# Query weights split over two DMA queues, keys and queries of two tiles up front, and x tile 2 loaded behind the weights

## Chip, cores, metric

One core of a Trainium2 chip runs the whole program. The metric is the device time of one execution in microseconds (us); a lower one is better. A profile is one execution; its times count from the start of the span. Most runs of one kernel agree within 0.3%, so a few tenths of a microsecond mean something only as a median over several runs.

The five engines here are TensorE (PE, matmuls; PEld is its weight load), VectorE (DVE), ScalarE (ACT), GpSimd (POOL) and SyncE (SP). Two of them issue DMA transfers (copies between memories, done by 16 DMA engines) in this kernel: SyncE, whose transfers the profile lists as queue q1, and ScalarE, queue q10.

## The reference

```python
# x: (1, 2048, 640) bf16, 32 heads of 20
g = sigmoid((x * gate_w).sum(-1))
q, k, v = split(x @ wqkv)                    # wqkv: (640, 1920)
phi = lambda t: where(t > 0, t + 1, exp(t)) + 1e-6
kv  = einsum(phi(k), v);  z = phi(k).sum over tokens
a   = (phi(q) @ kv) / (phi(q) . z + 1e-6) @ wo
b   = (gelu(x @ w_gate) * (x @ w_up)) @ w_down     # 1728 wide
out = g * a + (1 - g) * b
```

Only the first stage matters here: keys and queries of the 16 token tiles (128 tokens each), that is, x times wk and x times wq. Both weights are cut into five chunks of 128 rows (`k` = 0 to 4), 160 KB each. TensorE needs x transposed; tile 0 is transposed by TensorE, all the others by DMA on their way in.

## The kernel before

The start of the load program. Each operation is put on the queue of its engine in this order; waits are derived from what is read and written.

```python
NQ = 4        # tiles whose keys and queries are computed apart
...
load_x(0)                 # SyncE: x tile 0, plain
load_wk(0)                # SyncE
load_xT(1)                # SyncE: x tile 1, transposed by DMA
load_wk(3); load_wk(4)    # SyncE
load_wk(1, "act"); load_wk(2, "act")     # ScalarE
...
for i in range(2, NQ):    # SyncE: x tiles 2 and 3, transposed
    load_xT(i)
for k in range(KC):       # SyncE: wq, five chunks
    load_wq(k)
for i in range(NQ, NT):   # SyncE: x tiles 4 to 15, transposed
    load_xT(i)
# ... then plain x, gate and up weights, wv, wo
```

TensorE's program in the first stage: `KM(n, ks)` accumulates keys, `QM(n, ks)` queries, over the chunks `ks`, each chunk as two matmuls (512 and 128 or 129 columns). `seq` lists the keys of the NQ tiles, then their queries. After that `KQ(i)` does keys and queries of one tile together, three matmuls per chunk (512, 512, 257 columns). I call `KM`/`QM` the split form and `KQ` the fused form.

```python
warm(5, 512); warm(1, 128)               # matmuls on constants
T(0, [0], 7); T(0, [1, 2, 3, 4], 6)      # transpose x tile 0
warm(2, 128)
for k in range(3): KM(0, [k])
for k in range(3): KM(1, [k])
KM(0, [3]); KM(1, [3]); gate_col(); KM(0, [4]); KM(1, [4])
for n in range(2 * NQ):
    if n in (2, 3):
        KM(n, ALLK)                      # keys of tiles 2, 3
    if n == NQ:
        for k in ALLK:                   # queries of two tiles, chunk by chunk
            QM(NQ, [k]); QM(NQ + 1, [k])
    if n > NQ + 1:
        QM(n, ALLK)
    phi1(n); phi2(n)                     # ScalarE and VectorE
for i in range(NQ, NT):
    KQ(i)
    ...
```

## Time and profile before

| | before |
|---|---|
| time, median of 6 runs beside the change | 273.90 us (273.52 to 274.20) |
| span of the profiled run | 272.6 us |
| TensorE busy | 267.6 us (98%) |
| keys of tiles 0 and 1: first matmul / last ends | 4.45 / 7.7 us |
| key matmuls of tile 2 start | 8.12 us |
| first fused tile (tile 4) starts | 16.3 us |
| stage after the fused tiles starts | 48.80 us |

The page of the kernel before, its head, TensorE's line, and the chain of work that ended last:

```profile
span 272.6 us, 3416 instructions
...
PE 267.6 (98%) x1341; PEld 127.9 (47%) x1367; DVE 140.8 (52%) x247; ACT 75.9 (28%) x132; POOL 30.0 (11%) x28
...
PE 96%; DMA 1%; SPq 1%; issue 1%; DVE 0%
```

TensorE bounds the kernel. Its waits, from the list of who waited for whom (total us, times, longest us):

```profile
PE ps L419 <- PEq L914: 0.8, 1, 0.8
PE ps L453 <- DMA pool<-in_A_wqkv_dram: 0.5, 1, 0.5
PE ps L453 <- DMA pool<-in_A_x_dram: 0.4, 1, 0.4
```

That is all: the start, the first key weights, and a transposed tile of x. The timeline of TensorE around the last (start, duration, engine, line, operation; in brackets the idle time before it and what ended it):

```profile
7.27 0.38 PE L453 MATMUL ps<-pool 128*128 128x512 bf16 x1
7.49 0.22 PE L454 MATMUL ps<-pool 128*128 128x128 bf16 x1
8.12 0.39 PE L453 MATMUL ps<-pool 128*128 128x512 bf16 x1 [0.42 <-DMA pool<-in_A_x_dram]
```

The next key matmul would have started at about 7.55 us, one step of 0.06 after 7.49; it started 0.57 us later. This is what the change can win.

SyncE's queue in the same run (start and total duration of issue, merged):

```profile
3.06 1.04 SPq L341 DMA_DIRECT2D pool<-in_A_wqkv_dram  x2
4.14 2.53 SPq L353 DMA_TRANSPOSE pool<-in_A_x_dram  x2
6.72 2.48 SPq L341 DMA_DIRECT2D pool<-in_A_wqkv_dram  x5
9.24 16.34 SPq L353 DMA_TRANSPOSE pool<-in_A_x_dram  x12
```

The two transposes stand between wk's last chunks and wq. A semaphore event is the signal that a part of a load has landed, and each load here has 16. When a load landed is read from the last of them in the trace: wk's last chunk at 6.83 us, x tile 2 at 8.07, tile 3 at 8.77, wq at 9.40, 10.13, 10.55, 11.54, 12.05.

### The profile page before, as it was taken

The page shows a single profiled execution, that of the slowest core. Times are in us where ns is not written, and L with a number is a line of the kernel's source. Part 1 is how long each engine was busy: PE and PEld are TensorE (multiplying, and loading weights), DVE is VectorE, ACT ScalarE, POOL GpSimd, SP SyncE. Part 2 cuts the span into 40 slices and gives each one's busy share as a digit, 9 for nine tenths or more (in the row PEclk, how much of TensorE's full clock was granted, in tenths as well). Part 3 has the DMA queues.
Part 4 walks back from the last instruction along what each step waited for, and adds up shares of the span by engine and source line. Part 5 has one row for each costly group of instructions (what it writes and reads, how often), then busy time and mean ns, then how long its engine had stood idle before and what let it go on. Part 6 is the DMA issues. An engine that isn't in the chain of part 4 may idle for free.

```text
span 272.6 us, 3416 instructions
## 1 busy us (share of the span) xinstructions
PE 267.6 (98%) x1341; PEld 127.9 (47%) x1367; DVE 140.8 (52%) x247; ACT 75.9 (28%) x132; POOL 30.0 (11%) x28
## 2 busy tenths in 40 slices
PE   8999999999999999999999999999999999999997
PEld 3555555544445454444444444444444444444444
DVE  1678989997233335999999999634210000000200
ACT  2455555210422453232222233224011122121021
POOL 5000000003240002242332422000000000000000
DMA  7976999600200011514121221273031110110211
GB/s 192 202 115 127 346 399 388 140 2 19 58 19 2 23 50 51 192 34 49 26 48 25 49 48 27 60 219 105 5 77 38 41 38 19 38 41 19 58 58 41
DMA packets 42864, 23.78 MB, mean 87 GB/s; under 512 B 32223, under 2 KB 41439, under 8 KB 42719
## 3 DMA queue, kind: packets, MB, share of 16 engines
q1 hardware_dynamic: 42517, 23.22, 31.9%
q10 hardware_dynamic: 330, 0.33, 0.3%
q8 instruction: 11, 0.18, 0.3%
q14 instruction: 6, 0.05, 0.1%
HBM read 13.83 MB, written 2.63 MB: 60 GB/s over the span
## 4 chain that ended last, share of the span: by engine, by line
PE 96%; DMA 1%; SPq 1%; issue 1%; DVE 0%
PE ps L700 41%; PE ps L864 23%; PE ps L539 12%; PE ps L596 6%; PE ps L843 4%; PE ps L468 2%; PE ps L811 2%; PE ps L678 2%; PE ps L599 1%; DMA pool<-in_A_x_dram 1%; PE ps L453 1%; PE ps L824 1%; SPq L341 1%; PE ps L721 1%; SPq L353 0%
## 5 line engine op out<-in xcount | busy, mean ns | idle before, releaser
L700 PE MATMUL ps<-pool 128*128 128x512 bf16 x510 | 113.0, 379 | 0.5
L700 PEld LDWEIGHTS ps<-pool 128*128 128x128 bf16 x520 | 50.5, 98 | 60.0
L864 PE MATMUL ps<-pool 128*128 128x512 bf16 (+2 forms) x300 | 62.4, 366 | 0.3
L706 ACT ACTIVATE pool<-ps 128x512 f32<-128x512 f32 x52 | 31.0, 597 | 73.1 <-PE ps L700 73.1
L708 DVE TENSOR_TENSOR pool<-ps,pool 128x512 bf16<-128x512 f32 x52 | 34.7, 689 | 31.7 <-PE ps L700 30.4
L864 PEld LDWEIGHTS ps<-pool 128*128 128x128 bf16 x306 | 29.2, 98 | 33.4 <-issue 0.4
L847 DVE TENSOR_TENSOR pool<-ps,pool 128x512 bf16<-128x512 f32 x4 | 2.8, 690 | 61.5 <-PE ps L843 61.5
L539 PE MATMUL ps<-pool 128*128 128x512 bf16 (+1 forms) x176 | 32.5, 343 | 0.2
L754 POOL TENSOR_TENSOR pool<-pool 128x640 f32<-128x640 bf16 x16 | 22.4, 1404 | 73.0 <-DVE pool L756 65.6
L871 ACT ACTIVATE pool<-ps,pool 128x512 bf16<-128x512 f32 (+1 forms) x16 | 10.9, 680 | 68.6 <-PE ps L864 68.6
L539 PEld LDWEIGHTS ps<-pool 128*128 128x128 bf16 x180 | 17.6, 98 | 15.0
L558 DVE SCALAR_TENSOR_TENSOR pool<-ps,pool 128x128 bf16<-128x128 f32 (+2 forms) x36 | 21.7, 602 | 2.1
L549 ACT ACTIVATE pool<-ps 128x640 bf16<-128x640 f32 x24 | 16.9, 703 | 15.8 <-DVE pool L558 9.3
L596 PE MATMUL ps<-pool 128*128 128x512 bf16 x76 | 19.2, 379 | 0.1
L764 DVE TENSOR_TENSOR pool<-pool 128x640 bf16<-128x640 bf16 x16 | 13.2, 826 | 0.6
L762 DVE TENSOR_SCALAR pool<-pool 128x32 f32<-128x32 f32 x16 | 12.8, 802 | 0.6
L756 DVE TENSOR_REDUCE pool<-pool 128x32 f32<-128x640 f32 x16 | 12.9, 808 | 0.0
L644 DVE TENSOR_TENSOR pool<-pool 128x640 f32<-128x640 f32 x14 | 11.6, 826 | 0.5
L843 PE MATMUL ps<-pool 128*128 128x512 bf16 x51 | 11.5, 379 | 0.1
L646 POOL PARTITION_ALL_REDUCE pool<-pool x1 | 4.0, 3971 | 61.0 <-DVE pool L644 61.0
L596 PEld LDWEIGHTS ps<-pool 128*128 128x128 bf16 x78 | 7.0, 98 | 7.3
L555 DVE TENSOR_SCALAR pool<-pool 128x640 bf16<-128x640 bf16 x24 | 7.9, 327 | 1.7 <-ACT pool L549 0.4
(70 smaller groups left out, 124.1 us busy)
## 6 DMA issues: line engine op xcount, KB each, us to landing
out_dram<-pool SPq DMA_DIRECT2D x19, 128.0 KB, 1.7
pool<-in_B_w_gate_dram SPq DMA_DIRECT2D x1, 2080.0 KB, 14.8
pool<-in_B_w_up_dram SPq DMA_DIRECT2D x1, 2080.0 KB, 18.0
pool<-in_A_wqkv_dram SPq DMA_DIRECT2D x8, 160.0 KB, 3.1
pool<-in_A_x_dram SPq DMA_DIRECT2D x1, 1280.0 KB, 9.2
pool<-in_A_x_dram SPq DMA_DIRECT2D x1, 1120.0 KB, 6.3
pool<-in_B_w_down_dram SPq DMA_DIRECT2D x1, 1120.0 KB, 6.4
pool<-omg_row SPq DMA_DIRECT2D x1, 1024.0 KB, 4.8
```

Of the source, the lines that this page charges most:

```text
L539: last = e.matmul(ps[:, b + p, 0:c1 - c0], xT[:, k, i * 128:(i + 1) * 128], wkq[:, k, c0:c1], start=(k == 0), stop=(k == KC - 1))
L549: P.op("act", lambda e: e.activation(e_buf[m], ps_flat[:, o:o + 640], ACT.Exp), reads=banks, writes=[r_e[m]])
L558: P.op("dve", lambda e, c0=c0, c1=c1: e.scalar_tensor_tensor(dst[:, c0:c1], ps_flat[:, o + c0:o + c1], 1.0 + EPS, e_buf[m][:, c0:c1], ALU. ...
L596: last = e.matmul(ps[:, b, :], pk[i][:, c * 128:(c + 1) * 128], x_aug[:, i, 0:512], start=(i == 0), stop=(i == NT - 1))
L700: last = e.matmul(ps[:, b, :], w[:, k, fc * 128:(fc + 1) * 128], xT[:, k, j * 512:(j + 1) * 512], start=(k == 0), stop=(k == KC - 1))
L706: P.op("act", lambda e: e.activation(ge[n], ps[:, gb, :], ACT.Gelu_apprx_tanh), reads=[bank[gb]], writes=[r_ge[n]])
L708: P.op("dve", lambda e: e.tensor_tensor(hT[fc][:, j * 512:(j + 1) * 512], ps[:, ub, :], ge[n], ALU.mult), reads=[bank[ub], r_ge[n]], write ...
L754: P.op("pool", lambda e: e.tensor_tensor(tmp[n], pq[i], z_b, ALU.mult), reads=[r_pq[i], r_zb], writes=[r_tmp[n]])
L756: P.op("dve", lambda e: e.tensor_reduce(den[n], tmp[n].rearrange("p (h d) -> p h d", h=32), AX.X, ALU.add), reads=[r_tmp[n]], writes=[r_de ...
L764: P.op("dve", lambda e: e.tensor_tensor(pq[i].rearrange("p (h d) -> p h d", h=32), pq[i].rearrange("p (h d) -> p h d", h=32), den[n].unsqu ...
L843: last = e.matmul(ps[:, b, :], wd[:, fc, 512:640], hT[fc][:, j * 512:(j + 1) * 512], start=False, stop=(fc == NFC - 2), skip_group_check=True)
L864: last = e.matmul(ps[:, pb, 0:c1 - c0], lhs, rhs, start=False, stop=(q == len(rows) - 1), skip_group_check=True)
```

## The change

The intent: do not let the weights wait behind transposes. TensorE goes from the keys of tiles 0 and 1 straight to their queries, chunk by chunk as wq arrives; wq is issued from both queues at once so that it comes sooner; x tile 2 and all later tiles come behind wq and go through the fused form. (Tile 1 was transposed by DMA already before.)

```diff
-NQ = 4
+NQ = 2
...
-            for i in range(2, NQ):
-                load_xT(i)
-            for k in range(KC):
+            for k in (0, 2, 4):
                 load_wq(k)
-            for i in range(NQ, NT):
+            for k in (1, 3):
+                load_wq(k, "act", after=[r_wk[2]])
+            for i in range(2, NT):
                 load_xT(i)
...
             for n in range(2 * NQ):
-                if n in (2, 3):
-                    KM(n, ALLK)
                 if n == NQ:
                     for k in ALLK:
                         QM(NQ, [k])
                         QM(NQ + 1, [k])
-                if n > NQ + 1:
-                    QM(n, ALLK)
                 phi1(n)
                 phi2(n)
```

(`load_wq` gets the argument `after`, `load_wk` loses it.) `after=[r_wk[2]]` makes ScalarE wait until wk chunk 2 has landed before it issues chunks 1 and 3.

More of the change, by code (lines that the diff above doesn't have):

```diff
@@ L347, in load_x, with load_wk @@
                 dma_in(x_aug[:, i, 0:640], A_x[0, i * 128:(i + 1) * 128, :], [r_xn[i]], eng=eng)
-            def load_wk(k, eng="sp", after=()):
-                dma_in(wk[:, k, :], A_wqkv[k * 128:(k + 1) * 128, 640:1280], [r_wk[k]], reads=after, eng=eng)
+            def load_wk(k, eng="sp"):
+                dma_in(wk[:, k, :], A_wqkv[k * 128:(k + 1) * 128, 640:1280], [r_wk[k]], eng=eng)
             def load_xT(i, after=()):
@@ L355, in load_xT, with load_wq @@
                      reads=list(after), writes=[r_xT[i]], dma=new_dma_key())
-            def load_wq(k, eng="sp"):
-                dma_in(wq[:, k, 0:640], A_wqkv[k * 128:(k + 1) * 128, 0:640], [r_wq[k]], eng=eng)
+            def load_wq(k, eng="sp", after=()):
+                dma_in(wq[:, k, 0:640], A_wqkv[k * 128:(k + 1) * 128, 0:640], [r_wq[k]], reads=after, eng=eng)
             P.op("act", lambda e: e.dma_start(touch[0:16, 0:4], A_wqkv[0:128:8, 640:644]),
```

## The prediction

> **What bounds the kernel now.** TensorE: the page gives it 267.6 us busy of a 272.6 us span (98%), and the chain of waits is 96% TensorE. The list of TensorE's waits has three entries: 0.8 us at the start, 0.5 us for the first key weights, 0.4 us for tile 2 of transposed x. The clock was 1.00. Of these a reordering of loads can win back only the last: the keys of tiles 0 and 1 end at 7.7 us, the next start at 8.12 (timeline).
>
> **What the change removes, adds and moves.**
> - Arithmetic: none. Tiles 2 and 3 leave the split form (512+128 and 512+129 columns) for the fused one (512+512+257): the same 1281 columns per chunk, three matmuls instead of four. Timeline: split tiles take 2.73 us, fused ones 2.71 (12 in 32.5 us); two tiles save an estimated 0.05 us. The Trainium skill ("TensorE: Matmul & The Clock Gate", throughput formula) gives N/2.4 ns plus about 2.5 ns per matmul, so 0.025 us: the same order.
> - TensorE's need: before, tiles 2 and 3 of x at 7.7, then wq from 10.85 us. After, wq chunk 0 at 7.7 us and one more each 0.545 us, tile 2 at 10.45, tile 3 at 13.1.
> - Supply: before, two transposes (2.53 us of SyncE issue from 4.14 us) stood ahead of wq, which landed from 9.4 to 12.05 us (semaphore events). After, SyncE issues three chunks from 4.14 us at 0.5 us each, and ScalarE two, once wk chunk 2 has landed at 4.9. The DMA engines are 98% busy from 5 us, so issue is not the limit; the Trainium skill ("DMA: Bandwidth & Descriptors", "Issuing engines are not separate DMA queues") agrees that a second issuer saves only issue time. wk's last chunk landed at 6.83; a 160 KB chunk takes 0.5 to 0.6 us, so I estimate wq at 7.4, 8.0, 8.5, 9.1, 9.7 us, against need at 7.7, 8.25, 8.8, 9.35, 9.9: stall 0 to 0.3 us. Tile 2's packets then need 0.75 to 1.0 us and land 0.7 to 1.1 us after the last: 10.3 to 11. Stall 0 to 0.5 us.
>
> **On the critical path.** Removed: the 0.4 us wait, 0.05 us of matmul. Added: about 0.05 us for wq, 0.2 us for tile 2. Net about −0.25 us. VectorE is busy 3.66 of 4 us during fused tiles, yet TensorE shows no bank wait there; I expect none now. SyncE ends its transposes about 1.3 us earlier; nothing waits for what follows.
>
> **Predicted time 273.9 us, range 273.4 to 274.7.** Chances: faster by over 2% 0.005, within 2% 0.985, slower by over 2% 0.01.
>
> **What would show it.** In TensorE's waits the 0.4 us at 8.12 is gone; queries of tiles 0 and 1 start at 7.7 to 7.9 us; a wait there names a wqkv load and stays under 0.3 us; the first fused tile starts at 10.4 to 10.9 us, a wait before it naming x. Afterwards TensorE has no gap; fused tile 4 starts at 15.8 to 16.2 us against 16.3 before. ScalarE's wq issues appear at 4.9 us.
>
> **What would make it wrong.** The two issuers' chunks share the engines, so chunks 0 and 1 could both land near 8.1 us and delay the last key chunks too; then TensorE stalls 0.5 us or more and the change loses. Or transposes start slowly behind plain loads (a gap of nearly 3 us between two landings, 14.7 to 17.6 us, occurs in the trace before); on tile 2 or 3 it would cost 1 to 2 us.

## The result

| | before | after |
|---|---|---|
| time, median of 6 runs each | 273.90 us | 275.46 us (275.03 to 276.35) |
| ratio | | 1.0061 (95%: 1.0044 to 1.0079) |
| span of the profiled run | 272.6 us | 274.1 us |
| keys of tiles 0 and 1 end | 7.7 us | 8.0 us |
| queries of tiles 0 and 1 | 10.85 to 13.6 us | 7.81 to 12.3 us |
| first fused tile starts | 16.3 us (tile 4) | 12.34 us (tile 2) |
| stage after the fused tiles starts | 48.80 us | 50.26 us |

A ratio is the mean time of one kernel's runs over that of the other's of the same rounds, so it is not quite the ratio of the medians quoted.

The kernel is 1.6 us slower. The page after, its head, TensorE's line and the chain:

```profile
span 274.1 us, 3427 instructions
...
PE 268.8 (98%) x1357; PEld 127.5 (47%) x1357; DVE 140.9 (51%) x249; ACT 76.0 (28%) x132; POOL 30.0 (11%) x28
...
PE 96%; DMA 3%; ACTq 0%; DVE 0%; issue 0%
```

The share of TensorE says nothing: it is 98% in both. The list of its waits does:

```profile
PE ps L468 <- DMA pool<-in_A_wqkv_dram: 1.6, 1, 1.6
PE ps L419 <- PEq L910: 0.8, 1, 0.8
PE ps L453 <- DMA pool<-in_A_x_dram: 0.5, 1, 0.5
PE ps L453 <- DVE pool L437: 0.5, 1, 0.5
```

The last one is for the copy of the transposed tile 0, before the first keys. The wait of 1.6 us is new. Line 468 is the query matmul, so TensorE waited for a chunk of wq. The timeline shows which:

```profile
7.75 0.22 PE L454 MATMUL ps<-pool 128*128 128x128 bf16 x1
7.81 0.38 PE L468 MATMUL ps<-pool 128*128 128x512 bf16 x1
8.02 0.22 PE L469 MATMUL ps<-pool 128*128 128x129 bf16 x1
8.08 0.38 PE L468 MATMUL ps<-pool 128*128 128x512 bf16 x1
8.30 0.22 PE L469 MATMUL ps<-pool 128*128 128x129 bf16 x1
10.15 0.39 PE L468 MATMUL ps<-pool 128*128 128x512 bf16 x1 [1.63 <-DMA pool<-in_A_wqkv_dram]
```

The queries start without a wait, as soon as the keys are done. After one chunk (two tiles, two pairs of matmuls) TensorE stands until 10.15 us. It is chunk 1, the first of those issued from ScalarE. The queues of SyncE and of ScalarE after:

```profile
3.06 2.47 SPq L341 DMA_DIRECT2D pool<-in_A_wqkv_dram  x5
5.58 20.69 SPq L353 DMA_TRANSPOSE pool<-in_A_x_dram  x14
...
4.93 0.83 ACTq L341 DMA_DIRECT2D pool<-in_A_wqkv_dram  x2
```

Both issue as planned, and early. The semaphore events tell the rest. Chunks 0 to 4 landed at 7.13, **10.10**, 9.42, **10.84** and 10.59 us (bold: from ScalarE). Chunk 1 was issued at 4.93 us and took 5.2 us to land. The profile's list of DMA issues (`--dma`: KB each, median us from issue to landing) has it as a doubling of the ScalarE group's count with a longer median; before first, after second:

```profile
pool<-in_A_wqkv_dram ACTq DMA_DIRECT2D x2, 160.0 KB, 3.2
```

```profile
pool<-in_A_wqkv_dram ACTq DMA_DIRECT2D x4, 160.0 KB, 4.2
```

From the first fused tile on the two kernels run alike: 12 fused tiles took 32.50 us before, 14 took 37.92 after, 2.71 us per tile in both. So the loss arises in the first 12 us. From the last key pair to the first fused tile, the 0.57 us that TensorE lost before are gone, 1.8 us are lost instead (8.36, when the next query would have started, to 10.15), and the keys of this profile ended 0.26 us later, because tile 1 landed at 5.83 instead of 5.53 us. Tile 1 was issued before anything that the change touches, and landed between 5.40 and 6.04 us over the fourteen profiles, so I count that as chance. Together: 1.8 − 0.57 + 0.26 = 1.5 us, which is the difference of the spans.

### The profile page after: what moved, and what is told of

Read it like the earlier page. It is cut to its first block, busy times and chain, and to the rows that moved or that the text cites. A ratio compares the mean times of both kernels' runs of the same rounds, so it can differ in the third digit from the quotient of the medians.

```text
span 274.1 us, 3427 instructions
## 1 busy us (share of the span) xinstructions
PE 268.8 (98%) x1357; PEld 127.5 (47%) x1357; DVE 140.9 (51%) x249; ACT 76.0 (28%) x132; POOL 30.0 (11%) x28
## 4 chain that ended last, share of the span: by engine, by line
PE 96%; DMA 3%; ACTq 0%; DVE 0%; issue 0%
PE ps L696 41%; PE ps L860 23%; PE ps L535 14%; PE ps L592 6%; PE ps L839 4%; DMA pool<-in_A_wqkv_dram 3%; PE ps L674 2%; PE ps L807 2%; PE ps L595 1%; PE ps L820 1%; PE ps L468 1%; PE ps L717 1%; PE ps L735 0%; PE ps L469 0%; ACTq L341 0%; PE ps L602 0%
## 5 line engine op out<-in xcount | busy, mean ns | idle before, releaser
L696 PEld LDWEIGHTS ps<-pool 128*128 128x128 bf16 x520 | 50.5, 98 | 60.0
L860 PEld LDWEIGHTS ps<-pool 128*128 128x128 bf16 x306 | 29.2, 98 | 33.5 <-issue 0.4
L535 PE MATMUL ps<-pool 128*128 128x512 bf16 (+1 forms) x210 | 38.1, 344 | 0.0
L535 PEld LDWEIGHTS ps<-pool 128*128 128x128 bf16 x210 | 20.5, 98 | 17.5
L554 DVE SCALAR_TENSOR_TENSOR pool<-ps,pool 128x128 bf16<-128x128 f32 (+2 forms) x42 | 25.3, 602 | 2.8 <-DVE pool L551 0.5
L545 ACT ACTIVATE pool<-ps 128x640 bf16<-128x640 f32 x28 | 19.7, 704 | 17.9 <-DVE pool L554 11.2
L592 PEld LDWEIGHTS ps<-pool 128*128 128x128 bf16 x78 | 6.9, 98 | 7.2
L551 DVE TENSOR_SCALAR pool<-pool 128x640 bf16<-128x640 bf16 x28 | 9.1, 324 | 1.5
```

The costliest lines, as they stand in the source:

```text
L535: last = e.matmul(ps[:, b + p, 0:c1 - c0], xT[:, k, i * 128:(i + 1) * 128], wkq[:, k, c0:c1], start=(k == 0), stop=(k == KC - 1))
L545: P.op("act", lambda e: e.activation(e_buf[m], ps_flat[:, o:o + 640], ACT.Exp), reads=banks, writes=[r_e[m]])
L554: P.op("dve", lambda e, c0=c0, c1=c1: e.scalar_tensor_tensor(dst[:, c0:c1], ps_flat[:, o + c0:o + c1], 1.0 + EPS, e_buf[m][:, c0:c1], ALU. ...
L592: last = e.matmul(ps[:, b, :], pk[i][:, c * 128:(c + 1) * 128], x_aug[:, i, 0:512], start=(i == 0), stop=(i == NT - 1))
L696: last = e.matmul(ps[:, b, :], w[:, k, fc * 128:(fc + 1) * 128], xT[:, k, j * 512:(j + 1) * 512], start=(k == 0), stop=(k == KC - 1))
L860: last = e.matmul(ps[:, pb, 0:c1 - c0], lhs, rhs, start=False, stop=(q == len(rows) - 1), skip_group_check=True)
```

## Experiments

The question is why chunk 1 was late. Theory B: the weights cannot come sooner, whoever issues them. Theory R: two queues as such; their packets share the engines and get in each other's way. Theory T: the x transposes issued right behind wq on SyncE take the engines from ScalarE's chunks. Later, theory S: any traffic behind SyncE's chunks does so. A transfer at the start of a run comes some tenths earlier or later from run to run, so below the landing times are also given from the landing of wk's last chunk. All landing times are from one profile per kernel.

### SyncE alone (e1_sp_only)

```diff
-            for k in (0, 2, 4):
+            for k in range(KC):
                 load_wq(k)
-            for k in (1, 3):
-                load_wq(k, "act", after=[r_wk[2]])
```

> The kernel after, with all five wq chunks issued from SyncE in order 0 to 4 and none from ScalarE; everything else as after. Theory R (two issuers: chunks from two queues share the DMA engines, the engines drift apart, and chunk 1, issued from ScalarE, lands at 10.1 us): wq lands in order from about 7.1 to 9.7 us, TensorE waits under 0.3 us for wqkv, the first fused tile starts near 10.7, and the time is 1.5 us below after, about 0.1 to 0.4 us below before. Theory T (the x transposes issued right behind wq on SyncE overtake the ScalarE chunks and take engine time from them): the same, since behind wq in the same queue they cannot overtake. Theory B (800 KB of wq straight after wk need until about 10.5 us whoever issues them): a wait of 1 us or more stays and the time stays within 0.5 us of after.

Measured: the chunks landed in order, at 7.54, 8.51, 8.95, 9.48 and 9.92 us, and no wait for a query weight is left. Theory B falls. The time, though, was 275.12 us median of 6 (273.78 to 275.82), before 273.89 in the same rounds, ratio 1.0024 (0.9994 to 1.0054): no difference clear of the noise, and not the 273.5 to 273.8 expected. The profiled run, one of the four longer ones (275.1 to 275.8 us), shows another reason. Its waits and a stretch of TensorE's timeline:

```profile
PE ps L417 <- PEq L908: 0.8, 1, 0.8
PE ps L451 <- DMA pool<-in_A_wqkv_dram: 0.7, 1, 0.7
...
6.25 0.63 PE L451 MATMUL ps<-pool 128*128 128x512 bf16 x1
6.68 0.31 PE L452 MATMUL ps<-pool 128*128 128x128 bf16 x1
6.79 0.63 PE L451 MATMUL ps<-pool 128*128 128x512 bf16 x1
...
8.71 0.38 PE L451 MATMUL ps<-pool 128*128 128x512 bf16 x1
8.93 0.22 PE L452 MATMUL ps<-pool 128*128 128x128 bf16 x1
8.98 0.38 PE L451 MATMUL ps<-pool 128*128 128x512 bf16 x1
```

The key matmuls took 0.63 us and stepped at half speed (0.53 us per pair instead of 0.27) until 8.4 us; keys ended at 9.4 us instead of 7.7. In the profile of before this slow start ended at 5.3 us, in that of after it was over before the first key. The Trainium skill ("TensorE: Matmul & The Clock Gate", Part 1, on the clock gate) says that TensorE runs at half clock until it has been busy for about 3.4 us and that the length of this start varies from run to run; the traces agree on half speed and on the varying length (ending anywhere from before 4.4 to 9.6 us). They do not bear out the 3.4 us as a limit: in e3_sp_hold, below, the keys ran at half speed from 4.80 to 9.6 us without a gap. It is a second source of loss of over 1 us, and one profile can't tell it from the change's own. The next set therefore has a version with more warm-up.

### Transposes held, two queues (e2_hold) and SyncE alone (e3_sp_hold)

```diff
             for i in range(2, NT):
-                load_xT(i)
+                load_xT(i, after=r_wq if i == 2 else ())
```

on the kernel after, and on e1_sp_only.

> The kernel after with both queues, but the first transpose of x behind wq (tile 2, and so all the later ones) waits until all five wq chunks have landed. Theory R: with no transpose in flight chunk 1 still lands at 9 us or later, its 16 parts spread over 1.5 us or more, and TensorE's wait for wqkv stays above 1 us. Theory T: chunk 1 lands by 8.3 us and all of wq by 9.8 us; the wait for wqkv falls under 0.4 us. In both the wait for tile 2 grows: it lands about 3.5 us after the last chunk, near 13 us, so the time is above after, about 276 to 277 us.

> All five chunks from SyncE and tile 2's transpose held until wq has landed: the fourth corner. Theories R and T: wq lands as in the run with SyncE alone, within 0.3 us; the first fused tile waits for tile 2, which lands 3 to 3.5 us after the last chunk, near 13 us; time about 276 us. Theory B: last chunk at 10.5 us, tile 2 near 14 us, time about 277.

Measured: with two queues and nothing behind them, the chunks landed at 8.07, 9.60, 8.84, 10.05 and 9.79 us; TensorE waited 0.5 us for chunk 1. With SyncE alone: 7.46, 8.42, 8.86, 9.25, 9.64 us. From the landing of wk's last chunk, chunk 1 came after 1.94 us and 1.42 us. So with the transposes out of the way two queues cost chunk 1 some 0.5 us counted from wk, and 1.2 us counted from the start of the span (9.60 against 8.42). Of what was expected, two of R's three marks were met (chunk 1 after 9 us, its 16 parts spread over 1.8 us; the wait over 1 us was not) and none of T's (chunk 1 by 8.3, all of wq by 9.8, a wait under 0.4). Wk's last chunk came late in this run (7.66 instead of 6.70), and so the comparison from wk's landing was taken up, after this result was known. But 14 of that chunk's 16 parts had landed by 6.61 us, as in after (6.59): two late parts moved this zero, so it flatters the held run. Both counts are given below. The times, 276.27 (276.11 to 276.71) and 276.10 (275.67 to 276.81), are those of a late tile 2, as expected.

### Only the second queue added to before (e4_nq4_both)

The kernel before, with its two `wq` lines for one queue replaced by the three for two queues.

> The kernel before (four split tiles, tiles 2 and 3 of x ahead of wq) with only the second queue added: wq chunks 1 and 3 from ScalarE after wk chunk 2, the rest from SyncE. Theory R and T both say that the ScalarE chunks, issued at 4.9 us, now compete with the transposes of tiles 2 and 3: tile 2 lands at 8.5 to 9.5 us instead of 8.07 and TensorE's wait there grows from 0.4 to 1 us or more; time 0.4 to 1.2 us above before. If neither queue nor transposes matter: as before within 0.2 us.

Measured: 275.30 us (274.64 to 275.61), before 273.89, ratio 1.0036 (1.0008 to 1.0064). The second queue alone loses, with the old order of work. It was not tile 2 that came late (7.45 us) but tile 3, at 10.76 us instead of 8.77; TensorE stood 1.37 us for it. The ScalarE chunks landed at 9.28 and 10.54 us. The harm goes both ways: what ScalarE issues delays what SyncE had put in line, and its own chunks took 4.1 and 5.0 us from issue to landing.

### The clock's start taken out (f1_before_fill, f2_after_fill, f3_sp_fill)

```diff
             T(0, [1, 2, 3, 4], 6)
-            warm(2, 128)
+            warm(9, 128)
```

on before, on after, and on e1_sp_only.

> The kernel before with seven more warm-up matmuls of 128 columns (9 instead of 2) between the transposes of tile 0 and the first keys, so that TensorE has no idle stretch there. Theory C (two of the four profiles so far have key matmuls of 0.63 us instead of 0.38 until 8.4 or 9.5 us, after an idle stretch of 0.7 to 0.8 us before the first keys; this slow clock at the start is chance of the run and costs about 1.5 us wherever loads do not cover it): key matmuls take 0.38 us from 5.5 us on at the latest, the runs lie within 0.6 us of each other, and the median is 273.5 to 274.0. Rival (the slow start has another cause): slow runs of 275 us or more still occur.

> The kernel after with the same seven warm-up matmuls. Theory R (two queues make chunk 1 of wq late) together with C: the wait for wqkv of 1 to 1.8 us stays and the time stays at 275.0 to 275.6, since chunk 1 lands at about 10 us whether the keys were fast or slow. If the loss of after were the slow clock and not the loads, the time would fall to 273.5 to 274.

> All five wq chunks from SyncE, and the seven warm-up matmuls. Theories R and C: no wait for wqkv over 0.5 us, key matmuls of 0.38 us from 5.5 us on, the first fused tile starts at 10.5 to 11.2 us, and the runs lie at 273.2 to 274.0 us: 1.5 us under after and at or just under before. If the two-queue loading was not the cause: 275 us as after.

| | median, range of 5 runs | ratio to before (273.87) |
|---|---|---|
| f1_before_fill | 273.83 (273.74 to 273.89) | 0.9999 (0.9987 to 1.0012) |
| f2_after_fill | 275.33 (274.87 to 275.76) | 1.0056 (1.0044 to 1.0069) |
| f3_sp_fill | 274.08 (273.95 to 274.25) | 1.0009 (0.9995 to 1.0023) |

Without the scatter the verdict is plain: the change with two queues keeps its loss of 1.5 us, with one queue it is about 0.2 us above before (274.08, just over the 273.2 to 274.0 expected). The loss hangs on the second queue. About the clock the expectation was only half right: the runs are close together, but in the profiles of f2 and f3 the slow start still lasted until 6.7 us; the filling shortened it at most. In f2 chunk 1 landed at 10.44 us, as late as in after, though its keys had been slow; the wait was 1.3 us.

### Other chunks on ScalarE (f4_late_chunks)

```diff
-            for k in (0, 2, 4):
+            for k in (0, 1, 2):
                 load_wq(k)
-            for k in (1, 3):
+            for k in (3, 4):
                 load_wq(k, "act", after=[r_wk[2]])
```

> The kernel after, with chunks 0, 1, 2 from SyncE and 3, 4 from ScalarE in place of 0, 2, 4 and 1, 3: the same bytes on the same two queues, only other chunks. Theory R in the form that sharing makes the second chunk needed land among the last: chunk 1 now lands at 8.5 to 9.2 us, TensorE's wait for wqkv falls from 1.6 to 0.3 to 1.0 us in total, and the first fused tile starts at 11.3 to 11.9 us instead of 12.34; time 274.4 to 275.0. If two queues lower the rate of the engines as a whole, all chunks land at 10 to 10.8 us as before and the time stays at 275.3.

Measured: 275.50 us (275.30 to 276.09). Chunk 1 did land earlier (9.20 us) and its wait fell to 0.35 us, but TensorE then waited 0.48 us for chunk 2 and, by the profile, 0.97 us further on; the chunks landed at 7.83, 9.20, 10.40, 11.02 and 12.49 us. (The profile puts the last wait down to x, because tile 2 landed last; the matmul that waited is a query's, recorded at 12.76, after chunk 4. The record of the 512-column matmul just before it is missing, so the wait itself was shorter, an estimated 0.7 us from the end of the last matmul at 11.79 to chunk 4's landing.) The expectation of 274.4 to 275.0 is missed: choosing which chunk is late only moves the wait. The last chunk came 5.1 us after wk's last, against 2.4 us for the same two queues with nothing behind (e2_hold). That spoke for what comes behind, and against R as the whole cause.

### Plain loads behind instead of transposes (g1_plain_behind), and held once more (g2_fill_hold)

Both on f2_after_fill; g1 puts the plain 1120 KB load of x tiles 1 to 7 ahead of the transposes, g2 holds the transposes as e2 did.

> Two queues as after, with the seven extra warm-up matmuls, but SyncE issues the plain 1120 KB load of x tiles 1 to 7 between its wq chunks and the transposes, so that plain packets and no transposes run beside the two ScalarE chunks. Measured from the landing of wk's last chunk (in after: chunk 1 lands 3.4 us later, the last chunk 4.1). Theory T (transposes beside the ScalarE chunks hold the engines): chunk 1 at most 2.5 us and the last chunk at most 3.2 us after it. Theory S (any traffic on SyncE's queue behind its own chunks takes half the engines): chunk 1 at 3.0 us or more, the last at 3.8 us or more. Tile 2 comes late in both, so the time is no evidence: 278 us or more.

> Two queues, the seven extra warm-up matmuls, and the transposes held until all of wq has landed: the earlier hold run once more with a settled start. If traffic behind (of whatever kind) is what delays the ScalarE chunks: chunk 1 lands 1.5 to 2.3 us and the last chunk 2.0 to 2.8 us after wk's last, as in the earlier hold run and nearly as with SyncE alone (1.2 to 1.4 and 2.5 to 2.7). If two queues alone do it: chunk 1 at 3.0 us or more. Time near 276 us, from the late tile 2.

TensorE's longest wait in g1, then in g2 its wait for a query weight:

```profile
PE ps L468 <- DMA pool<-in_A_wqkv_dram: 2.9, 1, 2.9
```

```profile
PE ps L468 <- DMA pool<-in_A_wqkv_dram: 0.7, 1, 0.7
```

With plain loads behind it got worse, not better: chunk 1 came 4.4 us after wk's last chunk and the last chunk 5.3 us after it. Held, they came 2.3 and 2.7 us after. Theory T falls as far as it makes transposes special: plain loads behind do it too. Theory S stands, but as the table shows it is not all of the delay of chunk 1. (The times, 278.15 us for g1 and 276.32 for g2, are those of a late tile 2, as expected.) All profiles with the changed order together, in us after wk's last chunk, and in brackets from the start of the span:

| | queues | behind wq on SyncE | chunk 1 | last chunk |
|---|---|---|---|---|
| after | two | transposes | 3.40 (10.10) | 4.14 (10.84) |
| f2_after_fill | two | transposes | 3.67 (10.44) | 4.21 (10.98) |
| f4_late_chunks (chunk 1 from SyncE) | two | transposes | 1.80 (9.20) | 5.09 (12.49) |
| g1_plain_behind | two | plain x | 4.41 (11.13) | 5.31 (12.02) |
| e2_hold | two | nothing | 1.94 (9.60) | 2.39 (10.05) |
| g2_fill_hold | two | nothing | 2.26 (9.57) | 2.71 (10.02) |
| e3_sp_hold | SyncE | nothing | 1.42 (8.42) | 2.64 (9.64) |
| e1_sp_only | SyncE | transposes | 1.33 (8.51) | 2.74 (9.92) |
| f3_sp_fill | SyncE | transposes | 1.21 (8.48) | 2.54 (9.81) |
| g3_sp_only_again | SyncE | transposes | 2.03 (8.78) | 3.30 (10.04) |
| g4_sp_fill_again | SyncE | transposes | 1.21 (8.27) | 2.65 (9.71) |

On one queue what is behind makes no difference that stands out of the scatter. On two queues with nothing behind, all five chunks are there as soon as on one (2.4 to 2.7 us against 2.5 to 3.3), only chunk 1 is later: 9.57 and 9.60 us from the start of the span against 8.27 to 8.78.

How the delay of chunk 1 divides depends on the zero. From the start of the span the second queue by itself costs chunk 1 0.8 to 1.3 us, and traffic behind another 0.5 to 0.9 in the runs with transposes. From wk's landing the traffic behind is the larger share, but that zero hangs on late parts: in g2 too, 15 of the 16 had landed by 6.56 us and the last came at 7.31. So both parts are seen, and which is larger for chunk 1 stays open; for the last chunk it is the traffic behind by either count.

On two queues with traffic behind, the two ScalarE chunks share the engines first with SyncE's chunks and then with the transposes, which in one queue would have come after them. The packets show them side by side, though not on which engine: in g1, from 8.0 to 8.5 us the engines began 65 packets of 1280 bytes for SyncE's queue (SyncE's own chunks among them) and 60 for ScalarE's; in after, from 8.5 to 9.0 us, 50 for ScalarE's, 45 for SyncE's wq, and 122 transpose packets of 256 bytes. Such sharing with what is behind need not be all of it. The median packet of 1280 bytes took 55 ns (6 to 13 us), but in after two of SyncE's took 1.50 and 1.24 us, from 6.62 and 7.12 us on, before the first packet of the transposes behind (8.15 us). Such packets occur with one queue too (up to 1.08 us in e1); why, no run here shows.

### SyncE alone once more, without and with filling (g3_sp_only_again, g4_sp_fill_again)

> The SyncE-only kernel unchanged, on the same chip as its twin with the extra warm-up matmuls. Theory C (the slow start of the clock is what put four of its six runs at 275.1 to 275.8): runs fall into two groups, near 274.0 and near 275.2; the twin shows only the lower group. If the slow runs belonged to that chip, all runs are at 273.8 to 274.3.

> The SyncE-only kernel with the seven extra warm-up matmuls, beside the one without. All runs 273.8 to 274.4 us; no wait for wqkv over 0.5 us; the first fused tile starts within 0.3 us of the landing of tile 2's transpose, near 11.1 us, which is then what keeps it from beating before.

Measured: g3 274.14 us (five runs 273.71 to 274.29, one 276.71), ratio 1.0013 (0.9978 to 1.0048); g4 273.82 us (273.58 to 274.10), ratio 0.9990 (0.9961 to 1.0018); before 273.97, with one run of 276.03. In e1 four of six runs lay over 275 us; in its repeat, g3, one of six does. Whether filling prevents such runs stays open: none of 15 runs of the one-queue or old order with filling lay over 275 us; without it 5 of 12 one-queue runs did, but four of them in one set, and 3 of 37 runs of before. TensorE in g4:

```profile
10.24 0.38 PE L466 MATMUL ps<-pool 128*128 128x512 bf16 x1
10.45 0.22 PE L467 MATMUL ps<-pool 128*128 128x129 bf16 x1
10.84 1.46 PE L533 MATMUL ps<-pool 128*128 128x512 bf16 x6 [0.16 <-DMA pool<-in_A_x_dram]
```

Here the queries run through, and the first fused tile waits for tile 2, which landed at 10.70 us. The stage after the fused tiles starts at 48.75 us, against 48.80 before. This is what the change without the second queue does: it turns a wait of some 0.5 us for tile 2 after the keys into waits for wq's second chunk (none in e1 and g4, 0.51 us in g3) and for tile 2 after the queries (0.16 us in g4), and is worth nothing that can be measured.

## Why the prediction was wrong

- **What bounds the kernel**: right. TensorE, with only the first ten microseconds open to a change of loads, and all of the difference arose there.
- **The 0.4 us wait at 8.12 us goes away, and queries start at 7.7 to 7.9 us**: right (7.81 us).
- **Fused tiles keep their pace, VectorE makes no new wait**: right, 2.71 us per tile in both, no gap afterwards.
- **"a 160 KB chunk takes 0.5 to 0.6 us, so I estimate wq at 7.4, 8.0, 8.5, 9.1, 9.7 us"**: this step failed. It is a supply sum for one queue. For one queue it held within about half a microsecond: SyncE alone (e1) gave 7.5, 8.5, 8.95, 9.5, 9.9 us. With two queues it was 7.13, 10.10, 9.42, 10.84, 10.59, and the stall was 1.6 us where "0 to 0.3" had been said. The sum counted only the five chunks and had them land one after another in the order needed. Two queues did not keep that order: even with nothing behind, chunk 1 came at 9.57 and 9.60 us and TensorE waited 0.5 and 0.7 us for it. And the sum left out that SyncE's queue goes on after the chunks with 14 transposes, which in after run beside ScalarE's two chunks and no longer behind them; with them chunk 1 came at 10.10 and 10.44 us, with waits of 1.6 and 1.3 us.
- **"issue is not the limit"**, with the Trainium skill ("DMA: Bandwidth & Descriptors", "Issuing engines are not separate DMA queues"), which says that transfers of all issuers interleave on the same 16 engines and that a second issuer saves only issue time: true, and I drew half the conclusion. No gain was to be had from the second queue, but "interleave" also means that order is lost. The section on what would make it wrong named the sharing, yet between the chunks themselves and with 0.5 us; that part is what the held runs measured (0.8 to 1.3 us on chunk 1 from the start of the span, up to 1 us from wk's landing). The traffic behind, which it did not name, came on top.
- **Tile 2 lands at 10.3 to 11 us**: 11.35 us in after, too late to matter there; 10.70 to 11.08 with one queue. A net gain of 0.25 us had been expected from the reordering itself; with one queue it was 0.15 us in g4, −0.2 in f3 and g3, and −1.2 in e1 with its slow start, none clear of zero.
- **"SyncE ends its transposes about 1.3 us earlier"**: wrong and harmless. They ended at 26.3 us instead of 25.6; 14 took 20.69 us to issue, 1.48 each, where 12 had taken 1.36 each.

Shown: the second queue is the cause of the loss (in the times, f3, g3 and g4 against after and f2, and e4 on the old order; in the landings, e1 too), and part of it comes only with traffic behind on the first queue (e2, g2, g1). Open: how much of chunk 1's delay each of the two makes up, and where the single packets of over 1 us come from. Argued only: that the engines share packet by packet; the counts fit, but the arbiter itself isn't in the trace.

## What to carry to other kernels

When loads are needed in a certain order and the DMA engines are the limit, keep them on one queue in that order: here, moving some to a second queue broke the order by itself (chunk 1 about 1 us later with nothing behind) and let what was issued later on the first run beside them. A supply estimate must count all that is in flight next to a transfer and not only what stands ahead of it. And when a difference of 0.5% lies in the first microseconds, check the durations of single matmuls at the start before explaining it: here a slow start in some runs, over 1 us, was nearly as large as the effect.

## What the Trainium skill lacked or had wrong

- "DMA: Bandwidth & Descriptors", "Issuing engines are not separate DMA queues", says that a second issuer saves only issue time. It lacks that it can cost: moved to a second queue, with transposes behind on the first, chunk 1 landed at 10.10 and 10.44 us instead of 8.27 to 8.78, and the kernel lost 1.5 us.
- No page says how far the 16 engines drift apart in one transfer: the 16 parts of one 160 KB chunk landed within 0.3 us of each other in before at best (9.11 to 9.40 us), within 1.1 us for chunk 1 in e1_sp_only, but 3.5 us apart for chunk 1 in g1_plain_behind.
- "TensorE: Matmul & The Clock Gate", Part 1, says the slow start varies from run to run; the runs agree (it ended between before 4.4 and 9.6 us). It also warns that the clock events in a trace cannot be fully trusted, without naming the granted-clock column of such a profile; that column doesn't show the slow start: in e1_sp_only, between 4.6 and 8.2 us, it stood at 1.00 while the key matmuls stepped at half speed.
